# Raw weights fetched ahead of their decoding, staged copies one pair ahead, and a token mixing placed among the last pair's second layer

## The chip, the cores and the metric

The kernel runs on one core of a Trainium2 chip. The metric is the device time in microseconds (us). TensorE is called PE below, VectorE DVE, ScalarE ACT, GpSimd POOL, and SyncE, which issues all DMAs here, SP. Each engine works through its own queue in order.

## The reference

Three blocks follow one another on a batch of 4 sequences of 576 tokens with 512 features (8 heads of 64).

```python
phi(x): p = x @ w_phi; p -= max|p|; return concat(exp(p), exp(-p))        # 64 -> 256
attn:   num = phi(q) @ (phi(k)^T v); den = phi(q) . sum(phi(k)) + 1e-6; x = num / den
moe:    u = x + (x^T U V)^T ; x = u + relu(u @ w_ch1) @ w_ch2             # rank 32, hidden 2048
moe2:   u = x + (relu(x^T w_tok1) @ w_tok2)^T                             # token mixing, hidden 256
        out = u + relu(u @ w_ch1) @ w_ch2                                 # hidden 1536
```

The parameters of both moe blocks (U, V, the channel weights, the token weights) come as float64 and are held in DRAM as 64-bit integers.

## The kernel before

**Raw tiles.** `fetch64` (L142) loads a block of 64-bit words into a tile raw (two buffers, RAWB = 2) from SP's queue; `decode64` (L151) makes float32 of it with two ACT passes (L156 over the upper words, L157 over the lower ones into a tile r) and two DVE passes (L159, L162); the last of these is the last reader of raw. `load64` (L148) is fetch and decode in one call. A decoded block is split into a high and a low float32r part: a copy on ACT or DVE (L101, L103) and a subtraction on POOL or DVE (L106). Three matmuls (high by high, high by low, low by high) stand for one of full precision.

**Order of the work.** The kernel is written as Python loops, and a planner with a simulated time puts every engine's instructions into its queue: the order of the calls is a rank, and an instruction of low rank goes ahead of others where the planner thinks that it can start earlier. `tc.issue_after(x)` only keeps the instructions of its block behind x on the engine of x. Waits on buffers and data are real semaphores.

**Early stage (to about 350 us).** Rounds, registered with `at(r, ...)`, carry attention for 16 pairs of heads, five rounds a pair: `proj` (pp), `k1` and `k2` (kvp), `k3` (kvT copied on ACT, then transposed on PE as kvt), `q1` (transposes dT and exps qf), `q2` (nm), and the division. The first six pairs work in plain float32. Between them stand the decodes of the first six weight blocks of moe (12 halves, `fetch_wa` two rounds, L_WA, ahead of `load_wa`; from round O_WA on, every D_WA / 2 rounds), and U and V (`mix_u`, `mix_v`, each a load64 at a round of O_MIX). Channel work with those weights (hp_a, yp) begins at round 37.

**Middle stages.** The other ten hidden blocks of moe form five pairs (wB). `half_next` decodes one half of a block at a time, among the last channel work of the early stage and in chunk 0 of stage b. `channel` (L730) runs over five chunks of tokens (256, then four of 512 columns), first as stage b (moe's pairs), then as stage c (moe2's six pairs). For each pair p it makes the first layer (`one`, or `seven` with seven products X, Y, Z, V), then calls the hooks of p, then the second layer (`second`, 24 matmuls into four sums yp) of the pair before; the last pair's second layer ends the chunk, then VectorE adds yp to res and SP stores it. Hooks decode further weights: the token weights (`mix2_t1`, `mix2_t2`, nine pieces) in chunk 2, and moe2's channel weights (`decode`: 24 halves, each decoded and stored to DRAM, wD) in chunks 2 (four), 3 (ten) and 4 (ten). In chunk 4 `weights_c` (L911) also loads the first three pairs' halves back from wD into the staging tiles w, r and raw in turn, and splits them.

**Token mixing of moe2.** `tokmix2(b)` (L853) transposes five tiles of 128 tokens (x2p, two PSUM banks shared with first-layer sums), splits them (hhx, hlx), accumulates gp over the five, and after a relu makes eight products m2p that are added to x2 and stored. It is called for batches 0 to 2 after chunks 2 to 4 of stage b, and for batch 3 in chunk 0 of stage c (`last_mix`, behind the second layer of pair 0).

Of the kernel before, what the change touches and what calls it, by code (L numbers as in the profile page):

```python
# [19 lines left out]
P = 128  # L20
# [5 lines left out]
C = 512  # L26
# [54 lines left out]
O_TM = 12  # L81
M_AT = ((37, 59), (59, 81), (81, 100), (103, 118))
HELD = 7
O_MIX = (18, 20, 23)
O_WA = 4
D_WA = 5
L_WA = 2

# [6 lines left out]
def body(ctx, tc, kq, vd, w_phi, U, V, wm1, wt1, wt2, wm2, out):  # L95
# [53 lines left out]
        return decode64(fetch64(src, rows, n, name, copies), n, name)  # L149

    def decode64(raw, n, name):  # L151
        words = raw.bitcast(I32).rearrange("p (n two) -> p n two", two=2)
# [12 lines left out]
        return w  # L165
# [68 lines left out]
    US = ac.tile([P, NT, 4, 32], F32R, name="US")  # L234
    VS = ac.tile([P, S], F32R, name="VS")

    def mix_u():
        ur = load64(U, P, NT * 32, "u").rearrange("p (t r) -> p t r", r=32)
        cp("v", US[:, :, 0, :], ur)
        sub("v", US[:, :, 1, :], ur, f32(US[:, :, 0, :]))  # L240
        cp("v", US[:, :, 2:4, :], f32(US[:, :, 0:2, :]))

    def mix_v(k):
        sl = slice(k * N, (k + 1) * N)
        w = load64(V[:, sl], 32, N, f"v{k}", copies=4)
        cp("v", VS[:, sl], w)
        sub("v", VS[D:P, sl], w[D:P], f32(VS[D:P, sl]))

# [301 lines left out]
    for g in range(B * NPAIR):  # L550
        r = 5 * g
        at(r + O_LOAD, load, g)
        at(r + O_LOAD, load_v, g)
        at(r + O_VS, v_split, g)
        for i in range(NT):
            at(r + i, proj, g, i)
        for t in range(NT):
            at(r + t // 2 + O_K1, k1, g, t)
        for t in range(NT):
            at(r + t // 2 + O_K2, k2, g, t)  # L560
        at(r + O_K3 + (g < NF32), k3, g)
        for i in range(4):
            j, ch = i % 2, i // 2
            at(r + O_Q1 + ch, q1, g, j, ch)
            at(r + O_Q2 + ch, q2, g, j, ch)
        at(r + O_X0, x0, g)
        at(r + O_XR, xr, g)
        at(r + O_X1 - (g < NF32), x1, g)
    at(O_MIX[0], mix_u)
    for k in range(2):  # L570
        at(O_MIX[1 + k], mix_v, k)
# [52 lines left out]
    def put_half(w, W, k, i, el):  # L624
# [6 lines left out]
        else:  # L631
            for j, q in enumerate((6, 2)):
                split(w[:, j * 256 : (j + 1) * 256], sh[:, q], sl[:, q], "a", el)

    def half_next():
        if not halves or halves[0][0] not in wp:
            return
        p, k, i = halves.pop(0)
        if p not in wB:
            wB[p] = pair_tiles(p, "b")  # L640
        w = load64(wm1[NA + 2 * p + i][:, k * C : (k + 1) * C], P, C, f"b{2 * p + i}_{k}")
        put_half(w, wB[p], k, i, "p")

    for r in sorted(rounds):
# [15 lines left out]

    words = [(f, k) for p in range(NCP) for k in range(2) for f in (2 * p, 2 * p + 1)]

    def decode():
        if words:
            f, k = words.pop(0)
            sl = slice(k * C, (k + 1) * C)
            nc.sync.dma_start(wD[f][:, sl], load64(wm2[f][:, sl], P, C, f"c{f}_{k}"))

    wC = {}

# [59 lines left out]
    def channel(st, i, sl_, W, np_, src, plain, hooks):  # L730
# [65 lines left out]
            relu_split(ha, ah[:, h:], al[:, h:])  # L796
            return hs, relu_split(hb, bh, bl)

        def second(p, hs):
            vh, vl = W(p)[2:]  # L800
            for i, (hh, hl) in enumerate(hs):
# [6 lines left out]
        waiting = []  # L808
        for p in range(np_):
            hs, r = one(p) if plain else seven(p)  # L810
            if p == np_ - (2 if plain else 3):
# [22 lines left out]

    def mix2_t1(t):
        if not T:
            T["1"] = [tx.tile([P, NT, 256], F32R, name=f"T1{x}") for x in "HL"]
            T["2"] = [tx.tile([P, 2, S], F32R, name=f"T2{x}") for x in "HL"]
        w = load64(wt1[:, t], P, 256, f"t1_{t}")
        split(w, T["1"][0][:, t], T["1"][1][:, t], "a", "p")  # L840

    def mix2_t2(j, k):
        sl = slice(k * N, (k + 1) * N)
        w = load64(wt2[:, j, sl], P, N, f"t2_{j}_{k}")
        split(w, T["2"][0][:, j, sl], T["2"][1][:, j, sl], "a", "p")

    x2s = {}
# [5 lines left out]
    def tokmix2(b):  # L853
# [6 lines left out]
                nc.tensor.transpose(xp[:, c * P : (c + 1) * P], token_tile(x2, c, t), ident)  # L860
            return split_into(xp, *slot(f"x{b}_{t}"), t)

        ahead = [tokens(0), tokens(1)]
        for t in range(NT):
            xh, xl = ahead.pop(0)
            if t + 2 < NT:
                ahead.append(tokens(t + 2))
# [28 lines left out]
    def sums_b(p):  # L896
        return lambda: sums(p, wB[p])
# [6 lines left out]
    def loadc(f, j):  # L904
# [3 lines left out]
        nc.sync.dma_start(w, wD[f][:, j * C : (j + 1) * C])  # L908
        return w

    def weights_c(p):  # L911
# [14 lines left out]
    def wc_of(p):  # L926
# [1 line left out]

    hooksB = [
        {0: [half_b], 1: [half_b], 2: [sums_b(0)], 3: [sums_b(1)]},  # L930
        {0: [sums_b(2)], 1: [sums_b(3)], 2: [sums_b(4)]},
        {0: tt[:2], 1: tt[2:4], 2: tt[4:6], 3: tt[6:8] + dd, 4: tt[8:] + dd},
        {p: dd for p in range(NB)},
        {0: dd, 1: dd, 2: dd + [wc_of(0)], 3: dd + [wc_of(1)], 4: dd + [wc_of(2)]},
    ]
    for i, sl in enumerate(spans):
        channel("b", i, sl, wB.__getitem__, NB, u1D, i == 0, hooksB[i])
        if i >= 2:
            mix2_load(i - 2)
            tokmix2(i - 2)  # L940
    mix2_load(3)

    def last_mix():
        tokmix2(3)
        TX.close()
        wp[NB] = ctx.enter_context(tc.tile_pool(name=f"wp{NB}", **right))
        weights_c(NB)
# [69 lines left out]
```

## Time and profile before

| | us |
|---|---|
| median of 3 runs (lowest, highest) | 1044.17 (1043.98, 1046.59) |
| profiled execution, its own time | 1047.21 |
| its span | 1045.2 |
| PE busy (share of the span) | 1005.5 (96%) |
| DVE busy | 677.9 (65%) |
| ACT busy | 462.4 (44%) |
| POOL busy | 201.5 (19%) |

The span reaches from the first to the last instruction of the profiled execution; its own time is 2.0 us longer. Busy is the time in which an engine had an instruction under way; matmuls are pipelined, and their ends are modelled. The mean granted clock of the execution is 0.992 of full speed.

### The profile page before, as it was taken

The numbers are of one execution on the slowest core, as the hardware profiler recorded it, in microseconds if no ns is written. First come the engines' busy times: TensorE is split into PE (matmuls) and PEld (weight loads), VectorE is DVE, ScalarE is ACT, GpSimd is POOL, SyncE is SP. The second block draws the span as 40 slices with busy tenths as digits, with TensorE's granted clock in tenths as the row PEclk, the third lists the DMA queues.
The fourth block names the chain that finished last, engine by engine and source line by source line (L and its number), as shares of the span: only waits on it lengthen the run. The fifth ranks groups of instructions, "written<-read, shape, count | busy, mean of one in ns | idle before, by whom it ended". The sixth has DMA issues, their size and how long they took to land.

```text
span 1045.2 us, 16965 instructions
## 1 busy us (share of the span) xinstructions
PE 1005.5 (96%) x6436; PEld 910.8 (87%) x6436; DVE 677.9 (65%) x1267; ACT 462.4 (44%) x1091; POOL 201.5 (19%) x168
## 2 busy tenths in 40 slices
PE   7998999999999998999999999988999999999998
PEld 6876899999999888988987887976899898989897
DVE  5677887686767465597558657656578663544533
ACT  5767655655665556443336234344333231212211
POOL 2111455555455223300011000002210000000000
PEclk9999999999999999999999999999999999999999
DMA  6455412142221364531255756668513030120201
GB/s 196 128 145 155 132 56 78 51 129 56 67 91 47 97 204 149 182 102 41 82 189 182 244 180 201 213 182 269 183 47 102 1 116 6 37 86 1 82 1 41
DMA packets 79042, 118.87 MB, mean 114 GB/s; under 512 B 18160, under 2 KB 44528, under 8 KB 78960
## 3 DMA queue, kind: packets, MB, share of 16 engines
q1 hardware_dynamic: 78960, 117.78, 35.6%
q8 instruction: 51, 0.84, 0.3%
q14 instruction: 31, 0.25, 0.1%
HBM read 87.72 MB, written 29.96 MB: 113 GB/s over the span
## 4 chain that ended last, share of the span: by engine, by line
PE 70%; DVE 11%; DMA 10%; ACT 5%; issue 2%; POOL 0%; SPq 0%; DVEq 0%; ACTq 0%; POOLq 0%
PE yc L113 15%; PE yb L113 6%; PE hp_a L113 6%; PE yp L113 6%; PE pp L113 5%; PE nm L113 4%; PE kvp L113 4%; DMA raw_c<-in_wm_dram 4%; PE vc L113 3%; PE zc L113 3%; PE xc L113 3%; PE m2p L113 3%; DMA raw_b<-in_wm_dram 2%; PE xb L113 2%; PE vb L113 1%
## 5 line engine op out<-in xcount | busy, mean ns | idle before, releaser
L113 PE MATMUL yc<-hlc,vh_c 128*128 128x512 f32 (+1 forms) x240 | 88.1, 372 | 0.0
L113 PE MATMUL yc<-hhc,vl_c 128*128 128x512 f32 (+1 forms) x240 | 88.1, 372 | 0.0
L113 PE MATMUL pp<-KW,kq 128*128 128x256 f32 x320 | 83.5, 387 | 1.8 <-PE kvt L340 1.1
L113 PE MATMUL yc<-hhc,vh_c 128*128 128x512 f32 (+1 forms) x240 | 79.0, 372 | 0.0
L113 PE MATMUL yb<-hlb,vh_b 128*128 128x512 f32 (+1 forms) x200 | 74.2, 374 | 0.1
L113 PE MATMUL yb<-hhb,vl_b 128*128 128x512 f32 (+1 forms) x200 | 73.9, 372 | 0.0
L291 DVE TENSOR_REDUCE km<-pp 128x4 f32<-128x512 f32 x80 | 54.7, 684 | 25.7 <-PE pp L113 25.4
L113 PEld LDWEIGHTS pp<-KW,kq 128*128 128x128 f32 x320 | 57.9, 193 | 9.6 <-PE kvt L340 1.5
L113 PE MATMUL yb<-hhb,vh_b 128*128 128x512 f32 (+1 forms) x200 | 65.0, 378 | 0.9 <-ACT hhb L198 0.8
L106 POOL TENSOR_TENSOR qel<-qe,qeh 128x640 fp32r<-128x640 f32 (+1 forms) x40 | 58.7, 1479 | 30.5 <-DVE qeh L103 20.2
L113 PE MATMUL yp<-hha,wh_a 128*128 128x288 f32 x192 | 58.1, 305 | 2.5 <-ACT hha L198 2.4
L113 PE MATMUL hp_a<-uha,wh_a 128*128 128x288 f32 x192 | 59.1, 310 | 1.3 <-ACT uha L101 1.0
L113 PE MATMUL hp_a<-ula,wh_a 128*128 128x288 f32 x192 | 57.9, 302 | 1.8 <-DVE ula L106 1.8
L113 PE MATMUL hp_a<-uha,wl_a 128*128 128x288 f32 x192 | 57.9, 302 | 0.0
L113 PE MATMUL yp<-hha,wl_a 128*128 128x288 f32 x192 | 57.5, 301 | 0.0
L106 DVE TENSOR_TENSOR kd<-pp,km 128x512 f32<-128x512 f32 x80 | 54.9, 688 | 2.0
L113 PE MATMUL yp<-hla,wh_a 128*128 128x288 f32 x192 | 55.2, 300 | 0.5 <-DVE hla L199 0.5
L300 ACT ACTIVATE ke<-kd 128x256 f32<-128x256 f32 x80 | 33.6, 420 | 46.1 <-DVE kd L106 40.6
L113 PEld LDWEIGHTS yc<-hhc,vl_c 128*128 128x128 f32 x240 | 45.2, 188 | 7.3
L113 PEld LDWEIGHTS yc<-hlc,vh_c 128*128 128x128 f32 x240 | 45.3, 189 | 6.2
L106 POOL TENSOR_TENSOR kel<-ke,keh 128x512 fp32r<-128x512 f32 x30 | 39.6, 1325 | 46.4 <-ACT keh L101 41.0
L113 PEld LDWEIGHTS yc<-hhc,vh_c 128*128 128x128 f32 x240 | 42.6, 189 | 6.2
(303 smaller groups left out, 3014.0 us busy)
## 6 DMA issues: line engine op xcount, KB each, us to landing
raw_c<-in_wm_dram SPq DMA_DIRECT2D x24, 512.0 KB, 5.4
kq<-in_kq_dram SPq DMA_DIRECT2D x80, 128.0 KB, 2.4
raw_b<-in_wm_dram SPq DMA_DIRECT2D x20, 512.0 KB, 3.6
raw_a<-in_wm_dram SPq DMA_DIRECT2D x12, 512.0 KB, 4.6
wD<-w_c SPq DMA_DIRECT2D x24, 256.0 KB, 3.2
w_c<-wD SPq DMA_DIRECT2D x24, 256.0 KB, 3.7
rec<-rD SPq DMA_DIRECT2D x32, 144.0 KB, 3.4
u1D<-xT SPq DMA_DIRECT2D x8, 576.0 KB, 4.2
```

The costliest lines, as they stand in the source:

```text
L106: return ENG[e].tensor_tensor(out=o, in0=a, in1=b, op=ALU.subtract)
L113: return nc.tensor.matmul(o, l, r, start=start, stop=stop, skip_group_check=True)
L291: nc.vector.tensor_reduce(out=m, in_=pv, op=ALU.max, axis=AX.X, apply_absolute_value=True)
L300: exps.append(nc.scalar.activation(e[:, :, 0, :], d, AF.Exp).ins)
```

## The change

Raw tiles are fetched in their own calls, earlier in the order of the program, and kept in a list. For U and V the fetch stands two rounds ahead of the decode (`mix_fetch`), and both move to other rounds, as O_WA does. For all later weights one list, `stream`, holds the pieces in the order of their decoding, and `take` fetches until two are under way, decodes the first and fetches the next. Four halves of moe2's weights are decoded in chunk 1 of stage b, and chunk 4 decodes six in place of ten. The copies from wD of a pair are requested by `fetch_c` when the pair before has been split. `tokmix2` becomes a generator with three stops; `mixed_in` runs it in turn with the two halves of the last pair's second layer, and its remainder comes after the chunk's sums are stored. A batch's x2 is requested before its chunk.

```diff
-O_MIX = (18, 20, 23)
-O_WA = 4
+O_MIX = (20, 24, 27)
+O_WA = 6
...
+    def mix_fetch(i):
+        if i == 0:
+            rawM[0] = fetch64(U, P, NT * 32, "u")
+        else:
+            rawM[i] = fetch64(V[:, (i - 1) * N : i * N], 32, N, f"v{i}", copies=4)
     def mix_u():
-        ur = load64(U, P, NT * 32, "u").rearrange("p (t r) -> p t r", r=32)
+        ur = decode64(rawM.pop(0), NT * 32, "u").rearrange("p (t r) -> p t r", r=32)
...
-        w = load64(V[:, sl], 32, N, f"v{k}", copies=4)
+        w = decode64(rawM.pop(k + 1), N, f"v{k}")
...
+    for i in range(3):
+        at(O_MIX[i] - L_WA, mix_fetch, i)
...
+    def take():
+        while stream and len(flying) < RAWB:
+            src, n, nm = stream.pop(0)
+            flying.append((fetch64(src, P, n, nm), n, nm))
+        w = decode64(*flying.pop(0))
+        if stream:
+            src, n, nm = stream.pop(0)
+            flying.append((fetch64(src, P, n, nm), n, nm))
+        return w
     def half_next():
...
-        w = load64(wm1[NA + 2 * p + i][:, k * C : (k + 1) * C], P, C, f"b{2 * p + i}_{k}")
+        w = take()
...
+    stream += ws[:4] + ts[:6] + ts[6:8] + ws[4:6] + ts[8:] + ws[6:]
     def decode():
-        if words:
-            f, k = words.pop(0)
-            sl = slice(k * C, (k + 1) * C)
-            nc.sync.dma_start(wD[f][:, sl], load64(wm2[f][:, sl], P, C, f"c{f}_{k}"))
+        f, k = words.pop(0)
+        nc.sync.dma_start(wD[f][:, k * C : (k + 1) * C], take())
...
+        def mixed_in(p, hs, steps):
+            steps = steps()
+            next(steps)
+            for i in range(2):
+                second(p, hs, (i,))
+                next(steps)
+            rest.append(steps)
...
-                second(*waiting.pop(0))
-                hooks["flush"]()
-        if waiting:
+                mixed_in(*waiting.pop(0), hooks["flush"])
+                for _ in rest.pop():
+                    pass
+        if "tail" in hooks:
+            mixed_in(*waiting.pop(0), hooks["tail"])
+        elif waiting:
             second(*waiting.pop(0))
         for c in range(NC):
             nc.vector.tensor_add(res[:, c], yp[c][:, :n], res[:, c])
             nc.sync.dma_start((x2D if st == "b" else out)[:, c, sl_], res[:, c])
+        for steps in rest:
+            for _ in steps:
+                pass
     def tokmix2(b):
...
-        ahead = [tokens(0), tokens(1)]
+        xs = [tokens(0), tokens(1)]
+        yield
         for t in range(NT):
...
+            if t < 2:
+                yield
...
+    def fetch_c(p):
+        ahead[p] = [loadc(2 * p + i, k) for k in range(2) for i in range(2)]
     def weights_c(p):
         wC[p] = pair_tiles(p, "c")
-        for k in range(2):
-            for i in range(2):
-                put_half(loadc(2 * p + i, k), wC[p], k, i, "pv"[i])
+        for n, w in enumerate(ahead.pop(p)):
+            put_half(w, wC[p], n // 2, n % 2, "pv"[n % 2])
+        if p + 1 < NCP:
+            fetch_c(p + 1)
     hooksB = [
         {0: [half_b], 1: [half_b], 2: [sums_b(0)], 3: [sums_b(1)]},
-        {0: [sums_b(2)], 1: [sums_b(3)], 2: [sums_b(4)]},
+        {0: [sums_b(2)], 1: [sums_b(3)], 2: [sums_b(4)], 3: dd, 4: dd},
         {0: tt[:2], 1: tt[2:4], 2: tt[4:6], 3: tt[6:8] + dd, 4: tt[8:] + dd},
         {p: dd for p in range(NB)},
-        {0: dd, 1: dd, 2: dd + [wc_of(0)], 3: dd + [wc_of(1)], 4: dd + [wc_of(2)]},
+        {0: dd + [decode], 1: dd + [decode, lambda: fetch_c(0)], 2: [wc_of(0)], 3: [wc_of(1)], 4: [wc_of(2)]},
     ]
     for i, sl in enumerate(spans):
-        channel("b", i, sl, wB.__getitem__, NB, u1D, i == 0, hooksB[i])
         if i >= 2:
             mix2_load(i - 2)
-            tokmix2(i - 2)
+            hooksB[i]["tail"] = lambda b=i - 2: tokmix2(b)
+        channel("b", i, sl, wB.__getitem__, NB, u1D, i == 0, hooksB[i])
```

## Rows read from the trace of the kernel before

**Rows 1.** The page, part 1: busy us, share of the span, instructions.
```profile
PE 1005.5 (96%) x6436; PEld 910.8 (87%) x6436; DVE 677.9 (65%) x1267; ACT 462.4 (44%) x1091; POOL 201.5 (19%) x168
```

**Rows 2.** Windows: length, PE, PEld, DVE, ACT, POOL busy, granted clock, DMA.
```profile
0.00:25.00 25.00, 19.27 (x78) 15.46 (x79) 14.06 (x23) 13.64 (x34) 7.51 (x13) 0.93 0.69 200
75.00:100.00 25.00, 21.32 (x100) 17.34 (x99) 20.92 (x39) 18.23 (x47) 3.81 (x3) 0.93 0.51 146
500.00:525.00 25.00, 25.00 (x160) 22.61 (x160) 15.76 (x35) 8.44 (x20) 1.43 (x2) 1.00 0.35 117
875.00:900.00 25.00, 25.00 (x159) 22.46 (x158) 10.20 (x22) 4.98 (x12) 0.00 (x0) 1.00 0.00 1
...
350.00:445.00 95.00, 87.35 (x616) 83.09 (x615) 60.27 (x89) 53.40 (x110) 28.23 (x25) 0.96 0.53 169
550.00:590.00 40.00, 36.87 (x208) 31.19 (x207) 28.73 (x52) 17.71 (x37) 3.21 (x3) 0.96 0.61 207
675.00:760.00 85.00, 76.70 (x466) 65.63 (x465) 49.77 (x89) 34.85 (x70) 13.49 (x10) 1.00 0.62 202
```

**Rows 3.** PE's waits, 0 to 130 us: total, times, longest.
```profile
PE kvt L340 <- ACT kvT L101: 7.3, 2, 3.7
```

**Rows 4.** ScalarE's waits, 0 to 130 us.
```profile
ACT w_v L156 <- DMA raw_v<-in_V_dram: 6.7, 2, 3.7
ACT w_a L156 <- DMA raw_a<-in_wm_dram: 5.7, 5, 2.2
```

**Rows 5.** Timeline of ScalarE near 83 us: start, length, instruction, idle before.
```profile
83.35 0.46 ACT L156 ACTIVATE w_v<-raw_v 128x288 f32<-128x288 f32 x1 [3.74 <-DMA raw_v<-in_V_dram]
```

**Rows 6.** Timeline of PE near 83 us.
```profile
82.05 1.03 PE L113 MATMUL pp<-KW,kq 128*128 128x256 f32 x4
86.76 1.12 PE L340 MATMUL kvt<-ident,kvT 128*128 128x128 f32 x4 [3.68 <-ACT kvT L101]
87.67 1.91 PE L113 MATMUL pp<-KW,kq 128*128 128x256 f32 x4
```

**Rows 7.** One window behind that gap (columns of rows 2).
```profile
86.21:89.62 3.41, 2.86 (x9) 2.51 (x10) 3.32 (x7) 3.30 (x11) 0.00 (x0) 0.50 0.92 291
```

**Rows 8.** Timeline of ScalarE, 8 to 21.5 us.
```profile
16.91 0.67 ACT L156 ACTIVATE w_a<-raw_a 128x512 f32<-128x512 f32 x1 [1.71 <-DMA raw_a<-in_wm_dram]
18.02 0.80 ACT L101 CAST va<-vr 128x320 fp32r<-128x320 f32 x2
20.52 0.62 ACT L101 COPY kvT<-kvp 128x512 f32<-128x512 f32 x1
```

**Rows 9.** Waits of the SP queue, whole run.
```profile
SPq L145 <- DVE w_b L162: 58.3, 19, 4.5
```

**Rows 10.** PE's waits, 130 to 445 us.
```profile
PE yp L113 <- ACT hha L198: 2.4, 1, 2.4
```

**Rows 11.** The chain that ended last, 684 to 760 us: start, length, what.
```profile
688.21 7.88 DMA w_c<-wD
711.28 7.40 DMA raw_c<-in_wm_dram
```

**Rows 12.** ScalarE's waits, 665 to 730 us.
```profile
ACT vh_c L101 <- DMA w_c<-wD: 9.3, 4, 6.0
ACT w_c L156 <- DMA raw_c<-in_wm_dram: 8.1, 3, 4.1
```

**Rows 13.** PE's waits, 675 to 760 us.
```profile
PE xb L113 <- ACT eb L101: 1.9, 1, 1.9
PE gp L113 <- ACT hhx L367: 1.7, 1, 1.7
PE gp L113 <- DVE hlx L106: 1.2, 1, 1.2
```

**Rows 14.** PE's waits, 550 to 600 us.
```profile
PE gp L113 <- DVE hab L793: 1.0, 1, 1.0
```

**Rows 15.** The chain that ended last, near 618 us.
```profile
618.39 4.67 PE yb L113 x20
```

More of the change, by code (lines that the diff above doesn't have):

```diff
@@ L151, in decode64 @@
     def decode64(raw, n, name):
+        raw = raw[:, :n]
         words = raw.bitcast(I32).rearrange("p (n two) -> p n two", two=2)
@@ L235, in body @@
     VS = ac.tile([P, S], F32R, name="VS")
+    rawM = {}
+    def mix_fetch(i):
[3 more added lines that the diff above has]
+            rawM[i] = fetch64(V[:, (i - 1) * N : i * N], 32, N, f"v{i}", copies=4)
     def mix_u():
-        ur = load64(U, P, NT * 32, "u").rearrange("p (t r) -> p t r", r=32)
+        ur = decode64(rawM.pop(0), NT * 32, "u").rearrange("p (t r) -> p t r", r=32)
         cp("v", US[:, :, 0, :], ur)
@@ L633, in put_half @@
                 split(w[:, j * 256 : (j + 1) * 256], sh[:, q], sl[:, q], "a", el)
+    stream = [(wm1[NA + 2 * p + i][:, k * C : (k + 1) * C], C, f"b{2 * p + i}_{k}") for p, k, i in halves]
+    flying = []
+    def take():
[7 more added lines that the diff above has]
+        return w
     def half_next():
@@ L661, in body, with word @@
     words = [(f, k) for p in range(NCP) for k in range(2) for f in (2 * p, 2 * p + 1)]
+    def word(f, k):
+        return wm2[f][:, k * C : (k + 1) * C], C, f"c{f}_{k}"
+    t1s = [(wt1[:, t], 256, f"t1_{t}") for t in range(NT)]
+    t2s = [(wt2[:, j, k * N : (k + 1) * N], N, f"t2_{j}_{k}") for j in range(2) for k in range(2)]
+    ts, ws = t1s + t2s, [word(*x) for x in words]
+    stream += ws[:4] + ts[:6] + ts[6:8] + ws[4:6] + ts[8:] + ws[6:]
     def decode():
-        if words:
-            f, k = words.pop(0)
-            sl = slice(k * C, (k + 1) * C)
-            nc.sync.dma_start(wD[f][:, sl], load64(wm2[f][:, sl], P, C, f"c{f}_{k}"))
+        f, k = words.pop(0)
+        nc.sync.dma_start(wD[f][:, k * C : (k + 1) * C], take())
     wC = {}
@@ L797, in seven, with second @@
             return hs, relu_split(hb, bh, bl)
-        def second(p, hs):
+        def second(p, hs, which=(0, 1)):
             vh, vl = W(p)[2:]
-            for i, (hh, hl) in enumerate(hs):
+            for i in which:
+                hh, hl = hs[i]
                 for c in range(NC):
@@ L806, in second @@
                         mm(yp[c][:, :n], l, r, p == 0 and i == 0 and k == 0, p == np_ - 1 and i == 1 and k == 2)
-        waiting = []
+        def mixed_in(p, hs, steps):
[5 more added lines that the diff above has]
+            rest.append(steps)
+        waiting, rest = [], []
         for p in range(np_):
@@ L838, in mix2_t1 @@
             T["2"] = [tx.tile([P, 2, S], F32R, name=f"T2{x}") for x in "HL"]
-        w = load64(wt1[:, t], P, 256, f"t1_{t}")
+        w = take()
         split(w, T["1"][0][:, t], T["1"][1][:, t], "a", "p")
@@ L843, in mix2_t2 @@
         sl = slice(k * N, (k + 1) * N)
-        w = load64(wt2[:, j, sl], P, N, f"t2_{j}_{k}")
+        w = take()
         split(w, T["2"][0][:, j, sl], T["2"][1][:, j, sl], "a", "p")
@@ L861, in tokens @@
             return split_into(xp, *slot(f"x{b}_{t}"), t)
-        ahead = [tokens(0), tokens(1)]
+        xs = [tokens(0), tokens(1)]
+        yield
         for t in range(NT):
-            xh, xl = ahead.pop(0)
+            xh, xl = xs.pop(0)
             if t + 2 < NT:
-                ahead.append(tokens(t + 2))
+                xs.append(tokens(t + 2))
             for j in range(2):
@@ L909, in loadc @@
         return w
+    ahead = {}
+    def fetch_c(p):
+        ahead[p] = [loadc(2 * p + i, k) for k in range(2) for i in range(2)]
     def weights_c(p):
         wC[p] = pair_tiles(p, "c")
-        for k in range(2):
-            for i in range(2):
-                put_half(loadc(2 * p + i, k), wC[p], k, i, "pv"[i])
+        for n, w in enumerate(ahead.pop(p)):
+            put_half(w, wC[p], n // 2, n % 2, "pv"[n % 2])
+        if p + 1 < NCP:
+            fetch_c(p + 1)
     spans, t = [], 0
@@ L930, in body @@
         {0: [half_b], 1: [half_b], 2: [sums_b(0)], 3: [sums_b(1)]},
-        {0: [sums_b(2)], 1: [sums_b(3)], 2: [sums_b(4)]},
+        {0: [sums_b(2)], 1: [sums_b(3)], 2: [sums_b(4)], 3: dd, 4: dd},
         {0: tt[:2], 1: tt[2:4], 2: tt[4:6], 3: tt[6:8] + dd, 4: tt[8:] + dd},
         {p: dd for p in range(NB)},
-        {0: dd, 1: dd, 2: dd + [wc_of(0)], 3: dd + [wc_of(1)], 4: dd + [wc_of(2)]},
+        {0: dd + [decode], 1: dd + [decode, lambda: fetch_c(0)], 2: [wc_of(0)], 3: [wc_of(1)], 4: [wc_of(2)]},
     ]
     for i, sl in enumerate(spans):
-        channel("b", i, sl, wB.__getitem__, NB, u1D, i == 0, hooksB[i])
         if i >= 2:
             mix2_load(i - 2)
-            tokmix2(i - 2)
+            hooksB[i]["tail"] = lambda b=i - 2: tokmix2(b)
+        channel("b", i, sl, wB.__getitem__, NB, u1D, i == 0, hooksB[i])
     mix2_load(3)
     def last_mix():
-        tokmix2(3)
+        yield from tokmix2(3)
         TX.close()
```

## Prediction

> **What bounds the kernel now.** I read the page's busy times first: the matmul engine (PE) is busy 96% of a span of 1045.2 us [rows 1]. No matmul is added or taken away, so the change can only win PE's gaps and the time in which PE runs at half clock. The windows of 25 us say where these are [rows 2]. A stretch late in the last stage is full (25.00 of 25), so nothing can be won there. The first window has 5.7 us without a matmul; the one from 75 has 3.7; 350 to 445 has 7.65; 550 to 590 has 3.1; 675 to 760 has 8.3. Some of these windows also have a mean granted clock under 1. I then asked of each such stretch for whom PE waited, and followed the releaser one engine back. Every time it was ScalarE or VectorE, in-order engines that stood at a decode pass or a copy whose transfer had not landed.
>
> **U and V fetched two rounds before their decoding.** In the early stage PE waited twice for kvT, 7.3 us together, 3.7 the longest [rows 3]. ScalarE waited there 6.7 us in two waits for raw_v [rows 4]. The timeline joins the two: ScalarE's pass over raw_v starts at 83.35 after 3.74 us of idling for its transfer [rows 5], the copy kvT stands behind it in the same queue, and PE's transposes of kvT start at 86.76 after a gap of 3.68 us [rows 6]. Right behind, the stretch 86.21 to 89.62 has a granted clock of 0.50, which is the 1.2 GHz level of the two [rows 7]. Four pp matmuls take 1.91 us there and 1.03 just before the gap [rows 6]. That is 0.9 us for a third of the stretch; half of 3.41 us, 1.7, is the most that it can cost, and I take 1.5.
>
> The change splits load64 of U and V into a fetch at round O_MIX - 2 and a decode at O_MIX, as the first layer's weights already have it. Those waited 5.7 us in five times for 12 loads in the same stretch, mostly at the very start [rows 4], so a lead of two rounds is nearly enough. The fetches take the same SP queue earlier, nine DMA issues in all (one for U, four copies for each half of V), and the same two raw buffers: lead and decode of the fifteen pieces never need three at once by their round numbers. Gain: 3.68 + 1.5 = 5.2 at most, 0 at least (if a weight's load becomes the late one at that place). I take 5.
>
> **O_WA from 4 to 6.** The first gap, 7.3 - 3.7 = 3.6 us, has the same shape: kvT at 20.52 stands behind a pass over raw_a that began at 16.91 after 1.71 us of waiting, then casts of va and exps [rows 8]. With a start two rounds later one of two decodes (two passes of 0.67 us) leaves the place ahead of kvT. But its round number is only a rank: the planner puts passes into ScalarE's queue wherever it thinks the data has landed, and the loads still go out into the busiest DMA stretch; the remaining decode and va must wait for theirs. Ends: 0, and 3.6 + 1.5 = 5.1 if the gap and a stretch at half clock go (the window's mean clock is 0.93 [rows 2]). I take 1, near the two passes that move. The last weight decodes move by the same two rounds, towards a stretch where ScalarE and VectorE have more to do; they end at round 33, ahead of round 37 where they are first used, so I put nothing on it.
>
> **Raw loads two ahead (stream, take).** This looks like the main edit, and I cost it at 0. SP waited 58.3 us in 19 waits with a fetch (L145) for VectorE's last reader of a raw tile [rows 9]. So the loads of before are issued already as soon as one of the two raw buffers comes free, whatever their place in the program; take() uses the same two buffers (RAWB is 2) and its fetch waits for the same reader. Here the Trainium skill has a rule, "DMA: Bandwidth & Descriptors", section "Anatomy of one DMA — SWDGE (gpsimd) path", told there for GpSimd's queue: a DMA engine waits for no semaphore, the issuing sequencer does so before dispatch. By it a load named earlier only stands at SP's head for longer, and the sum for this edit is 0; the trace agrees (58.3 us of such waits). Were it otherwise, PE's wait for hha in the mixed stretch, 2.4 us [rows 10], and some 1.5 us of half clock behind it could go: 0 to 4. I take 0, since the row shows the buffer and not the order as the limit.
>
> **Decodes moved out of chunk 4, copies one pair ahead.** In chunk 4 before, each hook decodes two halves and three hooks also load and split a pair from wD, with staging tiles w, r and raw shared by both. The chain of waits runs there through transfers and not through PE: 7.88 us for a copy w_c, 7.40 us for a raw_c [rows 11]. ScalarE waited 9.3 us for copies in front of vh_c and 8.1 us for raw_c [rows 12]. PE paid with waits of 1.9 us for eb, 1.7 for hhx and 1.2 for hlx, 4.8 together, all of which stand behind such passes [rows 13]; its whole idle time from 675 to 760 is 8.3 [rows 2]. After the change four halves are decoded in chunk 1 and only six remain in chunk 4, in its first two hooks; each pair's four copies are requested a hook (a fifth of a chunk) before they are split. A hook's length is a pair's 42 matmuls of 256 and 24 of 512 columns; at 4.67 / 20 = 0.234 us for the longer [rows 15] and half of that for the shorter, 24 x 0.234 + 42 x 0.117 = 10.5 us (an estimate), against 7.88 for the slowest copy. Gain: 0 if PE only finds other releasers, 8.3 if all goes. Those of its gaps that belong to token mixing itself remain. I take 5.5: the 4.8 of the three rows and a small part of the rest.
>
> The price is in chunk 1: four decodes, each two passes of about 0.67 us on ScalarE and two as long on VectorE, some 5.4 us on either, and four stores on SP. The window there has 8.44 us of ScalarE and 15.76 of VectorE busy in 25 [rows 2], so both have room, but a relu can stand behind a pass. Ends: 0 (hidden) and 2.7 (each of four decodes delays one relu by one pass). I take 0.5.
>
> **Token mixing among the second layer.** Before, tokmix2 is called after the chunk; now its first two token tiles come ahead of the last pair's 24 matmuls of 512 columns, and its first two accumulation steps between and behind the two halves. Its 76 matmuls and 20 transposes for each batch are the same. From 550 to 590 PE idled 3.1 us [rows 2], the longest wait being 1.0 us at gp [rows 14], and the mean clock there is 0.96. Half a second layer, 12 matmuls of 0.234 us, is 2.8 us of cover for a split of a token tile on ScalarE and VectorE. Ends: a gain of 3.1 + 1.5 = 4.6 at the first of the four mixings, and the loss of the third rival. The planner has already put x2p and gp among second-layer matmuls in that trace, so I take 1.
>
> **The sum.** -5 - 1 - 0 - 5.5 + 0.5 - 1 = -12. The profiled execution took 1047.21 us, 2.0 around a span of 1045.2, and is 3.0 above the median of the runs, 1044.17. -12 makes 1035.2 of it, and 1032.2 of the median; I forecast **1032**.
>
> **Rivals.** *Much more goes.* If the start's gap goes with its slow stretch (5.1), the gap before yp with its own (4), and mixing gains 3 at the boundary, with 5 and 6 from the sure places: -23, 1021. For it: all these gaps have a landed-too-late transfer behind them. Against: three of them need an order in the queues that I can't read from before.
>
> *Nothing much.* The loads are held by two buffers and not by the program [rows 9]; if the same is true of the copies, and if at kvT a weight's pass waits in V's place, only some 2 us are won: 1042. For it: PE is busy 96% [rows 1], and a wait taken away from an in-order queue often uncovers the next one.
>
> *Slower.* PE takes its matmuls in the order written. In the four mixings gp steps now stand ahead of half a second layer that is ready. If ScalarE's hhx or VectorE's hlx come later than 2.8 us after the transposes, PE stops with ready work behind the stopped one; at one such place, hhx, it stopped 1.7 us before [rows 13], and slow clock can follow (1.5 us). There are eight such steps; at six of them, 6 x 3.2 = 19 us lost, against 12 won: 1051. It decides from four such steps on. For it: waits of gp are there in the trace of before already. Against: ScalarE has fewer passes with a late transfer in front. The Trainium skill says the same of the order ("PSUM — Partial Sum Buffer", section "Engine vs sequencer instructions": matmuls start and complete in program order); the trace agrees in that PE idled at gp [rows 13, 14], and where the queue had been free to choose this rival would fall away.
>
> **How the numbers follow.** About 0.3% (3.1 us) is what a measurement of this kernel can tell from no change. The forecast's own case, 7 to 18 us won (1026 to 1037), gets 0.50; more than that 0.17; 3 to 7 won 0.13; within 0.3% 0.11; slower 0.09. So faster 0.80, same 0.11, slower 0.09. The range 1020 to 1044 leaves out the slower case (0.09), the half of "same" above it (0.05) and a tail of the large gain (0.05).
>
> **What would show it.** No wait of ScalarE for raw_v or raw_u, and no 3.7 us gap of PE at kvT near 83 with a stretch at 0.50 behind; the first gap near 18 still there, a little shorter. SP's waits at the fetch still for VectorE's reader, and ScalarE's waits for raw_b in the mixed stretch about as before: if these vanish, my zero is wrong. In chunk 4 no wait for w_c or raw_c of several us, and PE's idle time there down from 8.3 to about 3. Chunk 1 still full. What would make the forecast wrong: new gaps at gp or yb in the tails, or new stretches at 0.50.

## The result and the profile after

| | before | after |
|---|---|---|
| median of 5 runs each, taken together (lowest, highest) | 1044.17 (1043.12, 1046.59) | 1051.05 (1047.64, 1052.97) |
| profiled execution, its own time | 1047.21 | 1048.97 |
| its span | 1045.2 | 1047.2 |
| mean granted clock | 0.992 | 0.996 |

The ratio after to before is 1.0053, 95% interval 1.0027 to 1.0078. I forecast 1032 and a range up to 1044; by this ratio the change made the kernel slower by 5.5 us (the two medians differ by 6.9).

Executions of one kernel differ by more than that (the kernel before ran from 1039.84 to 1050.76 us in one set of 33), so the two profiles alone can't carry the verdict; here before's own profile is one of its slower ones. They show where to look. First the page of after, part 1, beside [rows 1]:

```profile
PE 1003.2 (96%) x6436; PEld 907.7 (87%) x6436; DVE 682.1 (65%) x1267; ACT 462.5 (44%) x1091; POOL 204.5 (20%) x168
```

PE is busy 2.3 us less than in before, and the span is 2.0 longer: PE idles 44.0 us in place of 39.7. So over the whole execution the clock is not what was lost; it got better (0.996), and PE waits more. The windows of after say where; the columns are those of [rows 2]:

```profile
0.00:25.00 25.00, 21.14 (x90) 16.86 (x91) 15.22 (x25) 14.10 (x37) 5.81 (x12) 1.00 0.65 189
50.00:75.00 25.00, 21.49 (x96) 16.55 (x97) 18.52 (x32) 15.55 (x43) 2.53 (x2) 1.00 0.52 140
75.00:100.00 25.00, 23.42 (x118) 18.52 (x117) 20.44 (x37) 17.88 (x47) 5.08 (x4) 1.00 0.52 152
110.00:130.00 20.00, 16.45 (x100) 14.96 (x99) 19.11 (x30) 12.29 (x28) 13.64 (x9) 0.91 0.47 148
120.00:130.00 10.00, 7.70 (x43) 7.39 (x44) 9.21 (x14) 4.93 (x11) 7.95 (x6) 0.83 0.49 146
350.00:445.00 95.00, 86.02 (x617) 81.98 (x616) 57.42 (x87) 54.44 (x112) 27.97 (x25) 0.98 0.54 174
500.00:548.00 48.00, 46.19 (x290) 41.14 (x289) 33.28 (x68) 20.38 (x47) 2.91 (x4) 1.00 0.56 190
550.00:590.00 40.00, 36.42 (x208) 30.27 (x207) 27.94 (x51) 17.94 (x37) 3.22 (x3) 1.00 0.59 191
675.00:760.00 85.00, 79.72 (x474) 68.02 (x472) 51.35 (x82) 31.30 (x64) 13.57 (x10) 1.00 0.53 175
```

The stretch of V (75 to 100) is better by 2.1 us and runs at full clock, and chunk 4 (675 to 760) by 3.0, both as forecast in sign. But the stretch ahead of V's (50 to 75) lost 2.5, 350 to 445 lost 1.3, and chunks 1 and 2 (500 to 548) lost 1.8, where before was full. And from 110 to 130 PE lost 2.9 us where nothing was forecast; in the second half of that stretch it idles 2.3 of 10 us, at a mean clock of 0.83. Before has in these windows:

```profile
50.00:75.00 25.00, 23.95 (x114) 18.81 (x113) 17.94 (x35) 16.08 (x47) 3.81 (x3) 1.00 0.60 159
110.00:130.00 20.00, 19.30 (x129) 17.86 (x128) 18.97 (x32) 12.26 (x30) 12.17 (x10) 1.00 0.47 143
500.00:548.00 48.00, 48.00 (x291) 42.63 (x291) 28.69 (x60) 15.26 (x38) 4.51 (x6) 1.00 0.44 148
```

PE's waits from 105 to 130 us in after:

```profile
PE hp_a L113 <- DVE ula L106: 2.1, 1, 2.1
PE kvp L113 <- POOL kel L106: 0.9, 1, 0.9
PE mp L113 <- DVE xT L483: 0.5, 1, 0.5
```

Behind them stands a stretch at half clock (granted clock 0.50, the 1.2 GHz level):

```profile
124.76:128.17 3.41, 3.41 (x17) 3.39 (x17) 2.62 (x5) 1.80 (x3) 3.41 (x3) 0.50 0.56 184
```

VectorE's timeline in after shows what stood ahead of ula (the low part of the first channel work's input):

```profile
114.43 0.68 DVE L106 TENSOR_TENSOR kd<-pp,km 128x512 f32<-128x512 f32 x1
115.03 1.04 DVE L160 SCALAR_TENSOR_TENSOR w_a<-w_a,r_a 128x512 int32<-128x512 int32 x1
116.00 1.17 DVE L483 TENSOR_TENSOR xT<-mp,xT 128x288 f32<-128x288 f32 x3
117.09 0.42 DVE L103 CAST keh<-ke 128x512 fp32r<-128x512 f32 x1
117.43 1.76 DVE L163 SCALAR_TENSOR_TENSOR w_a<-raw_a,w_a 128x512 int32<-128x512 int32 x1
119.11 0.68 DVE L300 TENSOR_REDUCE km<-pp 128x4 f32<-128x512 f32 x1
119.71 0.44 DVE L483 TENSOR_TENSOR xT<-mp,xT 128x288 f32<-128x288 f32 x1
120.07 0.53 DVE L103 CAST wh_a<-w_a 128x512 fp32r<-128x512 f32 x1
120.53 0.44 DVE L483 TENSOR_TENSOR xT<-mp,xT 128x288 f32<-128x288 f32 x1
120.90 2.34 DVE L106 TENSOR_TENSOR ula<-xT,uha 128x1152 fp32r<-128x1152 f32 x1
```

There is no idle time in it: a late weight half (L160, L163 and the cast of wh_a, 3.33 us) is worked off ahead of ula, and PE's next hp_a starts at 123.29, when ula is done. In before, too, one half stands there:

```profile
113.32 0.68 DVE L159 SCALAR_TENSOR_TENSOR w_a<-w_a,r_a 128x512 int32<-128x512 int32 x1
114.04 0.70 DVE L162 SCALAR_TENSOR_TENSOR w_a<-raw_a,w_a 128x512 int32<-128x512 int32 x1
114.77 0.43 DVE L103 CAST wh_a<-w_a 128x512 fp32r<-128x512 f32 x1
121.37 1.35 DVE L106 TENSOR_TENSOR ula<-xT,uha 128x1152 fp32r<-128x1152 f32 x1
```

Counted from the span's start its ula even starts 0.5 us later, yet PE waits only 0.4 us for it, since PE itself came later in this execution: two of its stretches at half clock lie before 100 us, none of after's does. What after has more is this: the half ahead of the last one is decoded at 110.8 us in place of 99.2 (two passes, 1.4 us), the last half's own passes take 3.33 us in place of 1.81, and ula takes 2.34 in place of 1.35. That makes 3.9 us of VectorE (an estimate from these rows), more than half of it through passes of the same size that take longer; the last section shows what they stood beside.

### The profile page after: what moved, and what is told of

Its sections match the earlier page's. It is cut to its first block, busy times and chain, and to the rows that moved or that the text cites. A ratio compares the mean times of both kernels' runs of the same rounds, so it can differ in the third digit from the quotient of the medians.

```text
span 1047.2 us, 16964 instructions
## 1 busy us (share of the span) xinstructions
PE 1003.2 (96%) x6436; PEld 907.7 (87%) x6436; DVE 682.1 (65%) x1267; ACT 462.5 (44%) x1091; POOL 204.5 (20%) x168
## 4 chain that ended last, share of the span: by engine, by line
PE 61%; DVE 15%; DMA 15%; ACT 5%; issue 3%; SPq 0%; POOL 0%; DVEq 0%; ACTq 0%
PE yc L113 14%; PE hp_a L113 5%; PE yb L113 5%; PE yp L113 5%; PE pp L113 4%; PE nm L113 3%; PE kvp L113 3%; DMA raw_b<-in_wm_dram 3%; DMA raw_c<-in_wm_dram 3%; PE vc L113 3%; PE zc L113 3%; PE xc L113 3%; PE m2p L113 3%; PE gp L113 2%; DVE s L708 1%
```

## The experiments

The first theory after this comparison: the loss lies in the early rounds, at O_WA. Rivals: the new order in the chunks (the token mixing, as in my third rival, or the moved decodes), or a collision of parts that are harmless alone.

**One part alone**, the rest as before.

`only_rounds`: both constants and the early fetches of U and V.
```diff
-O_MIX = (18, 20, 23)
-O_WA = 4
+O_MIX = (20, 24, 27)
+O_WA = 6
+        at(O_MIX[i] - L_WA, mix_fetch, i)
```


> The kernel before with the rounds of the changed one alone: O_WA 6, O_MIX (20, 24, 27), U and V fetched two rounds ahead; all later loads, decodes, copies and the token mixing as before. Prediction's own view: 6 us faster (5 for V, 1 for the start). Theory after the result (the moved decodes cost more behind 104 us, where the profile of the changed kernel turns a lead of 2.5 us into a lag of 2.7 at 290, than they win at 83): 2 to 5 us slower. Rival (the loss lies in the later stages): at least 2 us faster.

`only_take`: stream and take in half_next, decode, mix2_t1 and mix2_t2, in the old order of decoding.
```diff
+        w = take()
+    stream += ts[:8] + ws[:2] + ts[8:] + ws[2:]
```


> The kernel before with stream and take alone, in the order of decoding of before. Prediction's own view: no difference (within 1.5 us), since two raw buffers hold the loads and not the program. Rival (fetches named earlier stand ahead of other transfers in SP's queue and make the decodes of chunk 2 later): 2 to 4 us slower.

`only_copies`: four decodes moved to chunk 1 and fetch_c one pair ahead.
```diff
+        {0: [sums_b(2)], 1: [sums_b(3)], 2: [sums_b(4)], 3: dd, 4: dd},
+        {0: dd + [decode], 1: dd + [decode, lambda: fetch_c(0)], 2: [wc_of(0)], 3: [wc_of(1)], 4: [wc_of(2)]},
```


> The kernel before with four halves decoded in chunk 1, six in chunk 4, and the copies from wD requested one pair ahead; loads with their decode as before. Prediction's own view: 5 us faster. From the profile of the changed kernel (1.2 us lost in chunk 1, 2 us won in chunk 4): about 1 us faster. Rival (a relu stands behind the decodes of chunk 1, and what chunk 4 wins is lost there): the same or 1 to 2 us slower.

`only_tail`: mixed_in and the generator tokmix2.
```diff
+            hooksB[i]["tail"] = lambda b=i - 2: tokmix2(b)
```


> The kernel before with the token mixing run among the last pair's second layer alone. Prediction's own view: 1 us faster. Theory after the result: within 1 us, since the profile of the changed kernel gains 1 us at the first boundary and nothing at the second. Rival (ready second-layer matmuls stand behind gp steps that wait): 3 us slower or more, with waits of PE at gp or yb in the tails.

| | median (lowest, highest) | ratio to before | interval |
|---|---|---|---|
| only_rounds | 1049.47 (1046.47, 1051.92) | 1.0039 | 1.0022 to 1.0055 |
| only_take | 1044.95 (1041.53, 1049.04) | 0.9999 | 0.9980 to 1.0018 |
| only_copies | 1046.11 (1043.12, 1050.29) | 1.0006 | 0.9988 to 1.0023 |
| only_tail | 1044.47 (1038.88, 1049.89) | 0.9989 | 0.9966 to 1.0012 |

Most of the loss comes with the rounds alone; the other three parts measure as nothing. The stretch of the loss in only_take, where the early queues are before's, against after's windows from 110 and from 120 to 130 above:

```profile
110.00:120.00 10.00, 9.32 (x67) 8.45 (x66) 9.97 (x20) 5.93 (x14) 7.21 (x7) 1.00 0.48 152
120.00:130.00 10.00, 10.00 (x74) 9.79 (x73) 9.08 (x14) 7.08 (x18) 6.90 (x5) 1.00 0.48 149
```

VectorE is as full (9.97 of 10), but in its order only one half stands ahead of ula there, ula starts at 116.54, and PE is full from 120 on.

**The rounds taken apart.** `rounds_wa` is before with `O_WA = 6` alone; `rounds_mix` has the new O_MIX and the early fetches alone; `wa_tail` moves only the last three of the twelve halves.
```diff
-        at(O_WA + (h * D_WA) // 2, load_wa, h // 2, h % 2)
+        r = O_WA + (h * D_WA) // 2 + 2 * (h >= 9)      # wa_tail; the fetch at r - L_WA
+        at(r, load_wa, h // 2, h % 2)
```
`own_buffer` keeps O_MIX but fetches U and V two rounds ahead into a raw tile of their own.
```diff
-        raw = stage.tile([P, 512], I64, tag="raw", name=f"raw_{name}")[:, :n]
+        raw = (pool or stage).tile([P, w], I64, tag=tag, name=f"raw_{name}")[:, :n]
```


> The kernel before with O_WA 6 alone; U and V as before. Theory 1 (the last weight decodes, two rounds later, meet the stretch from 100 to 130 us where VectorE's queue is already full, 9.97 of 10 us in one window): 2 to 4 us slower, with PE's waits at hp_a and kvp near 120, and the gap at kvt near 83 still there. Theory 2 (the whole loss is the weight load that the early fetch of U and V pushes back, ScalarE's 5.4 us wait for raw_a at 64): no difference or up to 1 us faster from the start.

> The kernel before with O_MIX (20, 24, 27) and U and V fetched two rounds ahead, O_WA at 4. Theory 2 (the early fetch holds one of the two raw buffers, so a load of a weight behind it goes out late): 1 to 3 us slower, with a wait of ScalarE for raw_a of several us near 60 to 70 in place of those for raw_u and raw_v. Theory 1: 1 to 3 us faster, the gap at kvt near 83 gone and nothing in its place.

> The kernel before with U and V fetched two rounds ahead of their old decode rounds (18, 20, 23) into a raw tile of their own, which takes none of the two that the weights use; O_WA at 4, all else as before. Theory 2: 2 to 4 us faster, no wait of ScalarE for raw_u or raw_v, no gap at kvt near 83 and no new wait for raw_a. If the waits at ScalarE were never worth anything to the end: the same as before.

> The kernel before with the last three of the twelve weight halves alone fetched and decoded two rounds later (26 to 28, 29 and 31 become 28, 31 and 33 or near). Theory 1: 2 to 3 us slower, like O_WA 6 as a whole, since only these meet the full stretch of VectorE. Theory 2: the same as before.

| | median (lowest, highest) | ratio | interval |
|---|---|---|---|
| rounds_wa | 1047.88 (1045.81, 1052.93) | 1.0028 | 1.0009 to 1.0047 |
| rounds_mix | 1043.94 (1040.36, 1047.23) | 0.9973 | 0.9954 to 0.9992 |
| own_buffer | 1046.79 (1044.01, 1050.43) | 1.0011 | 0.9990 to 1.0031 |
| wa_tail | 1047.87 (1045.74, 1053.23) | 1.0027 | 1.0006 to 1.0047 |

The last three halves alone make the loss of all twelve, and both traces have the 2.1 us wait for ula. The rounds of U and V gained 0.27% here. ScalarE's waits for raw tiles, 0 to 130 us, in rounds_mix:

```profile
ACT w_a L157 <- DMA raw_a<-in_wm_dram: 10.9, 5, 3.9
ACT r_u L158 <- DMA raw_u<-in_U_dram: 2.5, 1, 2.5
ACT r_a L158 <- DMA raw_a<-in_wm_dram: 1.1, 1, 1.1
ACT w_v L157 <- DMA raw_v<-in_V_dram: 0.9, 1, 0.9
```

V's wait went from 6.7 to 0.9, but the weights' went from 6.0 (the 5.7 of [rows 4] and 0.3 for r_a) to 12.0: the early fetch of U and V takes the raw buffer and SP's place that a weight had, and the weight is late instead. In after this is one long stall, seen in ScalarE's timeline and in PE's behind it:

```profile
59.05 0.64 ACT L101 COPY nd<-nm 128x256 f32<-128x256 f32 x2
65.02 0.68 ACT L157 ACTIVATE w_a<-raw_a 128x512 f32<-128x512 f32 x1 [5.33 <-DMA raw_a<-in_wm_dram]
```
```profile
64.82 0.63 PE L386 MATMUL dT<-ident,kd 128*128 128x128 f32 x4 [1.51 <-DVE kd L106]
68.08 0.66 PE L349 MATMUL kvt<-ident,kvT 128*128 128x128 f32 x4 [1.77 <-ACT kvT L101]
```

The buffer of their own did not help either. In own_buffer ScalarE's waits for raw tiles fall from 16.1 us in before (V 6.7, U 3.4, weights 6.0) to 6.7 (V 4.3, weights 2.4), not to nothing as I had expected, and the time stays; so these raw waits in themselves are not worth the 2 to 4 us that I had thought.

**The whole change without parts, and the other halves.** `mix_rest` is after with `O_WA = 4`; `no_rounds` is after with the old O_WA, O_MIX and load64 for U and V; `wa_head` is wa_tail's opposite (`2 * (h < 9)`), `wa_late` moves the last three halves by four rounds.

> The changed kernel whole, with only O_WA back to 4. Theory 1 (the loss comes from the last weight decodes, which stand two rounds later in VectorE's queue just ahead of ula; the rest is worth what it gave alone: U and V 0.27% faster, the other parts about nothing): ratio to before about 0.997, between 0.994 and 1.000; no wait of PE for ula of 2 us, no gap for kel of 0.9 us near 118, no half clock near 124; PE full from 110 to 130 but for small gaps. Theory 2 (parts that were neutral alone collide with each other, as U's fetch and the weights' did): the ratio stays at 1.003 to 1.006 and the time is lost after the early stage, or in it without O_WA. Theory 3 (the prediction's own sum, which had everything but 1 us of it outside O_WA): 0.990.

> The changed kernel with O_WA, O_MIX and the fetch of U and V as before: loads two ahead, the moved decodes and copies, and token mixing remain together. Theory 1 (loss and gain both lie in the rounds; these three parts add up as they did alone): 0.998 to 1.001; what chunk 4 wins (some 2 us) pays for chunks 1 and 2. Theory 2 (the three parts collide with each other): 1.003 or more, with PE's idle time in the chunks of stage b 3 us above before's. Theory 3 (the prediction's terms for chunk 4 and mixing): 0.994.

> The kernel before, with the first nine halves of the early weights two rounds later and the last three at their old rounds (the other half of O_WA). Theory 1 (only the last three cost): 0.998 to 1.001, VectorE reaches ula near 116 to 117 us and PE has no 2 us wait for it. Theory 2 (any shift of the weights' loads costs, because they meet V's): 1.002 to 1.003, with new waits for raw_a or raw_v between 20 and 90 us. The prediction's term for the start would show as 0.999, with the first gap at kvT gone.

> The kernel before, with the last three halves of the early weights four rounds later, where the kernel with two rounds lost 0.27%. Theory 1 (VectorE is full from 105 to 125 us, and each decode pass put ahead of ula and of the first hp_a delays PE): the loss grows, to 1.003 to 1.008, and PE's waits from 105 to 135 us grow beyond the 4 us with two rounds. Theory 2 (the loss is one collision at one place, and not VectorE's amount of work): it goes, 0.998 to 1.001, or stays at 1.003 with its waits elsewhere.

| | median (lowest, highest) | ratio | interval |
|---|---|---|---|
| mix_rest | 1045.53 (1042.61, 1048.45) | 1.0000 | 0.9987 to 1.0014 |
| no_rounds | 1043.54 (1040.67, 1046.37) | 0.9984 | 0.9971 to 0.9998 |
| wa_head | 1044.81 (1041.58, 1048.36) | 0.9993 | 0.9980 to 1.0006 |
| wa_late | 1048.72 (1047.28, 1050.32) | 1.0038 | 1.0024 to 1.0053 |

O_WA back at 4 takes the whole loss away, and the first nine halves alone cost nothing. Four rounds cost no less than two; whether more, 0.38 against 0.27%, the intervals leave open. In wa_late the wait for ula is gone, but the last half now stands at 128 to 133 us, and PE idles 4.05 us from 110 to 150 us in waits of 1.1 us and less:

```profile
110.00:150.00 40.00, 35.95 (x244) 33.18 (x243) 36.99 (x59) 24.42 (x60) 27.82 (x19) 1.00 0.42 123
```

The gain of U's and V's rounds is not there in mix_rest, which I had expected at 0.997. PE's waits in mix_rest, 105 to 130 us:

```profile
PE mp L113 <- DVE kd L106: 0.8, 1, 0.8
PE hp_a L113 <- DVE ula L106: 0.4, 1, 0.4
```

**Which halves collide with U and V.** `head_rest` is after with the last three halves at their old rounds (`- 2 * (h >= 9)`); `mix_head` is the same without the later stages' parts; `mix_tail` has instead the first nine at theirs.

> The changed kernel whole, with the last three of the twelve early halves back at their old rounds and the first nine still two rounds later. Theory 1 (the whole loss is the last three halves in VectorE's full stretch): 0.998 to 1.001, no 2 us wait for ula, no half clock near 124. Theory 2 (half of the loss is a collision of the first nine halves' loads with U's fetch in the two raw buffers): 1.002 to 1.003, with PE's waits near 64 to 68 us of 3 us and ScalarE's 5 us wait for raw_a as in the changed kernel.

> The kernel before, with U's and V's new rounds and fetches and the first nine halves two rounds later; the last three at their old rounds. Theory 1: 0.996 to 1.000, as the rounds of U and V gave alone. Theory 2 (the first nine halves collide with U's fetch): 1.001 to 1.003, the waits near 64 to 68 us as in the changed kernel.

> The kernel before, with U's and V's new rounds and fetches and only the last three halves two rounds later. Theory 1: 1.002 to 1.005, with the 2 us wait for ula. Theory 2: 0.999 to 1.001 (the sum of -0.27% and +0.27%), with the wait for ula but without those near 64 to 68 us.

| | median (lowest, highest) | ratio | interval |
|---|---|---|---|
| head_rest | 1045.90 (1042.89, 1048.43) | 1.0013 | 0.9998 to 1.0028 |
| mix_head | 1044.69 (1042.17, 1048.58) | 1.0004 | 0.9988 to 1.0020 |
| mix_tail | 1051.74 (1049.54, 1053.90) | 1.0068 | 1.0047 to 1.0088 |

The second theory (half of the loss from the first nine halves against U's fetch) falls: head_rest and mix_head keep ScalarE's wait for raw_a near 65 us (5.2 and 5.4 us) and lose little or nothing, while mix_tail, where it is 4.0, is the slowest of all. mix_tail was run 6 times, the other kernels of this section 11 or 12 times.

PE's gap itself tells the kernels apart. In all five with the last three halves two rounds late (after, only_rounds, rounds_wa, wa_tail, mix_tail) PE idles 3.5 to 3.6 us from 110 to 130 us, and ula takes 2.34 or 2.35 us; in the eleven with these halves whole and at their old rounds it idles 0.7 to 1.8.

**VectorE's passes of the last three halves cut to 16 of 512 columns** (the words of the other columns stay undecoded, so these kernels leave out work): `none_cut` on before, `tail_cut` on wa_tail, `after_cut` on after.
```diff
-            out=wi, in0=wi, scalar=3, in1=r, op0=ALU.logical_shift_left, op1=ALU.bitwise_or
+            out=wi[:, :m], in0=wi[:, :m], scalar=3, in1=r[:, :m], op0=ALU.logical_shift_left, op1=ALU.bitwise_or
```


> The kernel before, with the two VectorE passes of the last three early halves done over 16 of 512 columns only (the words of the others stay undecoded): 3.5 to 4 us less of VectorE in all. It is the control of the next run. Theory 1 (VectorE's passes cost where VectorE is full) and theory 2 (transfers, ScalarE passes or splits cost): 0.997 to 1.000 here.

> The last three early halves two rounds later, alone, with the same cut of their VectorE passes to 16 of 512 columns (the words of the others stay undecoded). Theory 1: as the control to 0.1%, 0.997 to 1.001; VectorE begins ula near 117 to 119 us in place of 121, and PE's wait for it is under 1 us. Theory 2: 1.002 to 1.003, with the 2 us wait.

> The whole change with the same cut of the last three early halves' VectorE passes (the words of the other columns stay undecoded). Theory 1: 1.000 to 1.002, near the whole change with these halves at their old rounds (1.0013). Theory 2: 1.004 to 1.006 as the whole change.

| | median (lowest, highest) | ratio | interval |
|---|---|---|---|
| none_cut | 1045.47 (1044.44, 1048.95) | 1.0004 | 0.9987 to 1.0021 |
| tail_cut | 1046.85 (1043.05, 1050.88) | 1.0020 | 1.0001 to 1.0039 |
| after_cut | 1046.88 (1043.65, 1051.23) | 1.0011 | 0.9993 to 1.0030 |

The window from 110 to 130 us, first of wa_tail, then of tail_cut:

```profile
110.00:130.00 20.00, 16.49 (x114) 15.13 (x113) 19.18 (x31) 12.23 (x28) 15.38 (x11) 1.00 0.50 156
```
```profile
110.00:130.00 20.00, 19.15 (x130) 17.53 (x129) 18.75 (x32) 13.88 (x32) 16.45 (x11) 1.00 0.55 170
```

PE gets 2.66 us back there, and ula starts at 118.45; in the whole change (after_cut, 19.14 busy) the loss falls from 0.53 to 0.11%, near head_rest's 0.13. So in the whole change these VectorE passes are most of it, with 0.3 of uncertainty on that difference. In tail_cut the time moved only from 0.27 to 0.20%: the trace is as theory 1 had it (PE waits 0.6 us for ula), the time at the low end of theory 2, and it decides nothing.

## Why the prediction was wrong

The contrasts that differ by one thing, in per cent of the time (differences of the ratios above, each uncertain by 0.2 to 0.3):

| what is added | in which company | change |
|---|---|---|
| last three halves late | alone; with U, V; with the first nine; with both; in the whole change | +0.27, +0.95, +0.35, +0.35, +0.40 |
| first nine halves late | alone; with the three; with U, V; with U, V and the three; in mix_rest | -0.07, +0.01, +0.31, -0.29, +0.13 |
| U and V early | alone; with nine; with three; with all twelve; in no_rounds | -0.27, +0.11, +0.41, +0.11, +0.16 |
| the three later parts | alone; with U, V; with U, V and nine; with only_rounds | -0.16, +0.27, +0.09, +0.14 |

Only the first row has one sign throughout; its mean is 0.46%, 4.8 us. The windows give the same size for after: from 110 to 130 us PE idles 3.55 us against 0.68 in only_take, 2.9 more, and half of the 3.41 us stretch at half clock is at most 1.7: 4.6 us. Of the five kernels with the late halves only after, only_rounds and rounds_wa have such a stretch near 124 us; wa_tail and mix_tail have none.

**O_WA is the step that failed**: "they end at round 33, ahead of round 37 where they are first used, so I put nothing on it". The weights did come in time. What came late was ula, which stands behind their passes in VectorE's queue just where VectorE is busy 19.1 of 20 us, and these passes and ula itself ran longer there (3.33 and 2.34 us against 1.81 and 1.35): PE waits 2.1 us for ula in place of 0.4. I had named the fuller stretch in the same paragraph and priced only the consumers of the moved weights, not those of the work they were put in front of. The gain of 1 us at the start can't be told from nothing: wa_head's 0.9993 has an interval from 0.9980 to 1.0006. PE's 5.7 us of idling in the first 25 us, where its gap lies, are 3.2 and 3.6 in no_rounds and only_take, which have the old rounds.

**U and V, -5.** The wait did vanish: near 83 us after has 1.01 and 0.23 us where before had 3.68. But the time did not follow. The five contrasts run from -0.27 to +0.41%, so the part is worth about nothing. The traces give three reasons. The gap was priced from one execution: no_rounds has the old rounds, and its two kvt waits are 4.0 us together, not 7.3 [rows 3]:

```profile
PE kvt L349 <- ACT kvT L101: 4.0, 2, 2.8
```

The gap also moved more than it went: PE idles 3.5 us from 50 to 75 us in after and 2.9 to 4.0 in all kernels with the early fetches, against 0.8 to 3.1 in those without. And the lower end that I gave ("if a weight's load becomes the late one at that place") is what happened, 12 us of waits for raw_a in rounds_mix. My sentence that the fifteen pieces "never need three at once by their round numbers" was no proof against it, since a buffer is held from its fetch on, and SP stands in order. The 1.5 for the half clock comes out much the same (0.88 x 3.41 / 1.91 = 1.6), though its reading was off: the four matmuls fill 1.91 of the 3.41 us, over half of the stretch and not a third.

**Loads two ahead, 0**: right within only_take's interval (0.9999, 0.9980 to 1.0018). SP's wait at the fetch is still for VectorE's last reader: the row of [rows 9] is 58.8 us in after against 58.3, and the loads of moe2's weights now wait there as well:

```profile
SPq L145 <- DVE w_b L163: 58.8, 19, 6.5
SPq L145 <- DVE w_c L163: 89.3, 20, 25.1
```

In before SP waits for w_c at the store of the decoded half (L667, 38.2 us) and has no such row at the fetch. ScalarE's waits for raw_b did not vanish either: 12.6 us from 350 to 455 us, 10.0 in before.

**Decodes and copies, -5.5 and +0.5.** Chunk 4 has 3.0 us less of PE's idle time in after (8.3 to 5.3), but that is no proof of a gain: before's 8.3 is the largest of all twenty kernels, and mix_head, whose chunk 4 is before's, idles only 5.0 there (at 0.98 of the clock):

```profile
675.00:760.00 85.00, 79.96 (x481) 68.95 (x480) 49.84 (x91) 34.00 (x68) 13.43 (x10) 0.98 0.62 201
```

ScalarE's waits for w_c and raw_c did not go, 17.7 us together where before has 21.5; 665 to 730 us in after, beside [rows 12]:

```profile
ACT r_c L158 <- DMA raw_c<-in_wm_dram: 9.7, 4, 6.5
ACT sh_c L101 <- DMA w_c<-wD: 4.7, 2, 3.9
ACT vh_c L101 <- DMA w_c<-wD: 3.3, 3, 1.9
```

PE found other releasers, as the low end of that term had it; 675 to 760 us, where gp and xb [rows 13] are gone and yb, 0.5 us in before, has grown:

```profile
PE yb L113 <- DVE hlb L200: 1.8, 2, 1.0
PE yb L113 <- ACT hhb L199: 1.3, 3, 0.6
```

The price in chunk 1, put at 0.5, is 1.8 over 500 to 548 us, where the four decodes also push the token weights later; ScalarE waits 6.0 us for raw_t there. This loss recurs: in every kernel with decodes in chunk 1 PE idles 0.5 to 1.9 us in that window, in every other one not at all. Net, of the two profiles: 1.2 of 5. only_copies and only_tail each leave it at nothing, and the three later parts together at -0.16% (0.02 to 0.29) in no_rounds, 1.7 us where I had 6.

**Token mixing, -1**: 0.9989, within its interval of 1. From 550 to 590 PE is busy 0.45 us less than in [rows 2], and the mean clock is 1.00 in place of 0.96; its waits for gp there are 2.4 us against 2.5.

**The rivals.** "Slower" had the right sign and the wrong place: in chunk 4 no wait for gp is left in after. "Nothing much" named the right mechanism, one queue's wait uncovering the next.

**What stays open.** Why the three halves cost 0.95% beside U's and V's rounds and 0.27% alone; why tail_cut kept most of its loss although PE's gap had closed; and whether the gain of rounds_mix alone is real, since four other contrasts deny it. no_rounds (0.9984) and rounds_mix (0.9973) are the only versions whose whole interval lies below 1, and by little.

## What to carry to other kernels

When work moves in in-order queues, price it where it lands: look up the windows of the engines there, and ask which instruction is now behind it, not only who uses its result. A stall that is read from one execution needs a second one before it is priced, and a fetch that is moved ahead into the same few buffers makes another fetch late. A sum of gains of about 0.5% and less should have been checked against the spread of single executions.

## What the runs showed of the hardware

Stretches of 3.41 us at half clock come and go between kernels whose early queues are alike: before and no_rounds have one near 86 us, only_take has none in the first 370 us; before has five ahead of the span's end, after two, mix_rest one, though after is the slowest of the three. So a stretch seen in one execution is a poor term for a sum.

VectorE's passes with two inputs from SBUF took longer where they began beside a subtraction of GpSimd, by about as much as that had still to run and not in proportion to their own size (the profile's spans on GpSimd are rough). In tail_cut two passes of the same 16 columns took 0.17 and 0.88 us in VectorE's timeline; GpSimd's timeline has a subtraction that ends within 0.03 us of the longer one (113.04 + 1.28 = 114.32, and 113.47 + 0.88 = 114.35):

```profile
109.89 0.17 DVE L160 SCALAR_TENSOR_TENSOR w_a<-w_a,r_a 128x16 int32<-128x16 int32 x1
113.47 0.88 DVE L160 SCALAR_TENSOR_TENSOR w_a<-w_a,r_a 128x16 int32<-128x16 int32 x1
```
```profile
113.04 1.28 POOL L106 TENSOR_TENSOR wl_a<-w_a,wh_a 128x512 fp32r<-128x512 f32 x1 [5.40 <-ACT wh_a L101]
```

The same is seen at full size in after, beside VectorE's timeline above. GpSimd's timeline:

```profile
117.18 1.46 POOL L106 TENSOR_TENSOR kel<-ke,keh 128x512 fp32r<-128x512 f32 x1
120.75 1.27 POOL L106 TENSOR_TENSOR wl_a<-w_a,wh_a 128x512 fp32r<-128x512 f32 x1 [0.43 <-PE mp L113]
```

The pass L163, begun at 117.43, ends 0.55 us behind the first of these (119.19 against 118.64), and ula, begun at 120.90, ends 1.22 behind the second (123.24 against 122.02); in before they took 0.70 and 1.35 in all. This is regular: before and after together have 48 such passes of 512 columns over the twelve early halves. The 41 that began while GpSimd had nothing under way took 0.68 to 0.70 us; the other seven took 0.80 to 1.76 us and each ended 0.55 us behind GpSimd's instruction. The instruction beside ula is the split of the late half itself, so this half costs ula time on GpSimd's side too.

So the cut did not take away all that a late half costs VectorE, which may be why tail_cut kept loss; that was not tried. The Trainium skill ("GPSIMD Engine Reference", section "1. Specifications") says that GpSimd shares its SBUF interfaces with VectorE and contends with VectorE's instructions that are in a 2-port performance mode or have two SBUF inputs; the passes above have two, and their rows agree.
